# Float64 weights split from the upper word alone, magnitudes made one piece ahead, and layer 1's sets of seven products in another order

## The chip, the cores and the metric

The kernel runs on one core of a Trainium2 chip. The metric is the device time of one execution in microseconds (us), median of three runs. Five engines matter: TensorE (PE, the matmuls, and PEld, its weight loads), VectorE (DVE), ScalarE (ACT), GpSimd (POOL) and the DMA queue of SyncE (SP). Each engine takes its own instructions in the order in which the program was written, and waits on semaphores where it needs another engine's result.

## The reference

```python
attn_out = retention(q, k, v)              # float32, 4 x 8 heads x 576 x 64
x = attn_out as (2304, 512)
h = x @ moe_w_in                           # float64 weights, 512 x 2048
x = (max(h, 0) ** 2) @ moe_w_out           # the first block: float64 weights, 2048 x 512
p = probs / (probs.sum(-1) + 1e-9)         # 2304 x 4
out = sum over e of p[:, e] * (max(x @ w1[e], 0) @ w2[e])   # the second block, float32 weights
```

Matmul operands are float32 numbers held as a high and a low part (names ending in `hi` and `lo`), and every product is three matmuls: high by high, high by low, low by high.

## The kernel before

Three stages follow each other: attention (0 to 79 us), the first block (79 to 520 us) and the second block. The change touches the first block alone.

**Chunks and jobs.** The first block takes the 2048 hidden columns in eight chunks `c` of 256 (`NW1`). The 2304 tokens stand in five groups `g`, four of 512 and one of 256. A list `jobs`, written out by hand, gives the order: a layer 1 job for chunk and group, then the layer 2 jobs of an earlier layer 1 (`behind`). Layer 2 (`layer2_1`) multiplies the hidden values `ghi`/`glo` by `w2hi`/`w2lo` into a bank `o` and VectorE adds that to the sums `y` (L860).

**Sets of seven.** For chunks 2 to 5 (`sevens`) two groups of 512 tokens (a pair) go through layer 1 together as a two-by-two block product with seven instead of eight products (`layer1_seven`). Each chunk has two such calls, eight in all. A product is six matmuls of 512 columns (L658). The seven results stand in four PSUM banks `b1`, `b6`, `b7`, `b5`; `b1`, `b7` and `b5` each take a second product on top of the first one. Before that, the first result must have been read: `b1` by ScalarE's copy to `u[0]` (L677), `b7` and `b5` by VectorE's `add` (L666). At the end of each of the four sums stands `square`: Relu (L589) and Square (L591) on ScalarE, then `split`: ScalarE's copy to the high part (L123) and GpSimd's subtraction for the low part (L124).

**Weights in the background.** The weights of the first block arrive as float64. Each chunk has eight pieces of 128x256 doubles: four for layer 1 (`split_w1`) and four for layer 2 (`split_w2`). `load_piece` fetches them into three rotating buffers `wraw`. `from_f64` turns one piece into `hi` and `lo`: Abs of the upper word on ScalarE (L105), four VectorE operations on the exponent (L107 to L113), a fifth that scales the lower word (L115), GpSimd's sum of the two (L116), then `split`. In chunks 2 to 5 `split_w1` also makes the four sums S1 to S4 of the quarters A11 to A22 that the seven products need.

These are Python generators in a list `work`. After every product and every layer 2 tile, `tick(n)` runs `n` steps of the first generator, a step being the code between two `yield`s. That alone decides where a step's instructions stand in each engine's queue. `combine`, which makes four differences of the tokens (T1 to T4) for each pair and saves them to memory, is a generator in the same list, during chunks 0 and 1. Before a job, `drain` runs whatever is left of the weights that the job needs. `pull` issues the loads that bring the saved differences back (L611).

Of the kernel before, what the change touches and what calls it, by code (L numbers as in the profile page):

```python
# [28 lines left out]
BC = 256  # L29
# [4 lines left out]
def tile_kernel(ctx, tc, qT, kT, kn, vn, v4d, mask, qdec, kdec, wd, w, probs, probs2, out, outT):  # L34
# [33 lines left out]
    def f32(ap):  # L68
        return ap.bitcast(F32)
# [20 lines left out]
            nc.sync.dma_start(out=r, in_=w[(c - NW1) % NW2][:, 2 * BC * i : 2 * BC * (i + 1)])  # L90
        wraw[c, i] = r

    def from_f64(r, hi, lo):

        n = r.shape[1]
        low, high = r[:, :, 0], r[:, :, 1]
        m = cvp.tile([128, n], I32, name="cv_m", bufs=4)  # L100
        p = cvp.tile([128, n], F32, name="cv_d", bufs=2)
        a = m.bitcast(F32)
        v = nc.vector
        yield
        nc.scalar.activation(out=a, in_=high.bitcast(F32), func=ACTF.Abs)  # L105
        yield
        v.tensor_scalar(out=a, in0=a, scalar1=2.0**-15, scalar2=2.0**16 * 1.875, op0=ALU.max, op1=ALU.min)  # L107
        yield
        v.tensor_scalar(out=m, in0=m, scalar1=5, scalar2=2, op0=ALU.logical_shift_left, op1=ALU.logical_shift_right)
        yield  # L110
        v.scalar_tensor_tensor(out=m, in0=high, scalar=-(1 << 30), in1=m, op0=ALU.bitwise_and, op1=ALU.bitwise_or)  # L111
        yield
        v.tensor_scalar(out=p.bitcast(I32), in0=m, scalar1=-(1 << 23), scalar2=None, op0=ALU.bitwise_and)  # L113
        yield
        v.scalar_tensor_tensor(out=p, in0=low.bitcast(U32), scalar=2.0**-52, in1=p, op0=ALU.mult, op1=ALU.mult)  # L115
        nc.gpsimd.tensor_tensor(out=a, in0=a, in1=p, op=ALU.add)  # L116
        yield
        yield
        split(a, hi, lo)
        return a  # L120

    def split(src, hi, lo):
        nc.scalar.copy(out=hi, in_=src)  # L123
        nc.gpsimd.tensor_tensor(out=lo, in0=src, in1=f32(hi), op=ALU.subtract)  # L124
# [7 lines left out]
    def split_w1(c):  # L132

        hi = wp.tile([128, 8 * BC], F32R, name="w1hi")
        lo = wp.tile([128, 8 * BC], F32R, name="w1lo")
        blk = [slice(BC * i, BC * (i + 1)) for i in range(8)]
        if c < NW1:

            w1s[c] = [t.rearrange("p (i k m) -> p i k m", i=8, k=2) for t in (hi, lo)]
            u, v = {}, nc.vector  # L140
            for i, to in ((2, A21), (3, A22), (0, A11), (1, A12)):
                r = wraw.pop((c, i))
                u[to] = yield from from_f64(r, hi[:, blk[to]], lo[:, blk[to]])
                load_piece()
                if c not in sevens:
                    continue
                if to == A11:
                    yield
                    v.tensor_tensor(out=u[A22], in0=u[A21], in1=u[A22], op=ALU.add)
                    yield  # L150
                    v.tensor_tensor(out=u[A21], in0=u[A11], in1=u[A21], op=ALU.subtract)
                    split(u[A22], hi[:, blk[S1]], lo[:, blk[S1]])
                    yield
                    v.tensor_tensor(out=u[A11], in0=u[A22], in1=u[A11], op=ALU.subtract)
                    split(u[A21], hi[:, blk[S3]], lo[:, blk[S3]])
                    yield
                    split(u[A11], hi[:, blk[S2]], lo[:, blk[S2]])
                if to == A12:
                    yield
                    v.tensor_tensor(out=u[A12], in0=u[A12], in1=u[A11], op=ALU.subtract)  # L160
                    yield
                    split(u[A12], hi[:, blk[S4]], lo[:, blk[S4]])
            return
        w1t[c] = hi, lo
        w1s[c] = [t.rearrange("p (i k m) -> p i k m", i=8, k=2) for t in (hi, lo)]
        r0, r1 = wraw.pop((c, 0)), wraw.pop((c, 1))
        a11, a12, a21, a22 = r0[:, :BC], r0[:, BC:], r1[:, :BC], r1[:, BC:]
        v = nc.vector
        s = [cvp.tile([128, BC], F32, name="cv_m", bufs=4) for _ in range(4)]
        todo = [  # L170
            (s[0], a21, a22, ALU.add), (s[1], s[0], a11, ALU.subtract), (s[2], a11, a21, ALU.subtract),
            (s[3], a12, s[1], ALU.subtract),
        ]
        src = {A11: a11, A12: a12, A22: a22, A21: a21, S1: s[0], S2: s[1], S3: s[2], S4: s[3]}
        for i in (A11, S2, S3, A12, S1, A22, S4, A21):
            for _ in range(2 if todo else 0):
                yield
                o, x, y, op = todo.pop(0)
                v.tensor_tensor(out=o, in0=x, in1=y, op=op)
            yield  # L180
            split(src[i], hi[:, blk[i]], lo[:, blk[i]])
            if i in (A12, A21):
                load_piece()
# [12 lines left out]
    def split_w2(c):  # L196

        whole = NW1 <= c < NW1 + NW2 - 1
        new_w2(c, whole)
        blk = lambda y, i: w2b(c, y, i, i + 1)  # L200
        if c < NW1:
            for i in range(4):
                r = wraw.pop((c, 4 + i))
                yield from from_f64(r, blk(0, i), blk(1, i))
                load_piece()
            return
        r = wraw.pop((c, 2)), wraw.pop((c, 3))
        a = [r[i // 2][:, BC * (i % 2) : BC * (i % 2 + 1)] for i in range(4)]
        v = nc.vector
        t = [cvp.tile([128, BC], F32, name="cv_m", bufs=4) for _ in range(4)]  # L210
        todo = [
            (t[0], a[H21], a[H22], ALU.add), (t[1], t[0], a[H11], ALU.subtract), (t[2], a[H21], a[H11], ALU.subtract),
            (t[3], a[H12], t[1], ALU.subtract),
        ]
        for piece in ((H11, H21), (H12, H22)):
            for i in piece:
                yield
                split(a[i], blk(0, i), blk(1, i))
            for _ in range((3 if piece[0] == H11 else 1) if whole else 0):
                yield  # L220
                o, x, y, op = todo.pop(0)
                v.tensor_tensor(out=o, in0=x, in1=y, op=op)
            load_piece()
        for i in range(4 if whole else 0):
            yield
            split(t[i], blk(0, 4 + i), blk(1, 4 + i))
# [298 lines left out]
    with tc.manual_schedule():  # L525
# [62 lines left out]
        def square(h, r, hi, lo, act=True):  # L588
            nc.scalar.activation(out=r, in_=h, func=ACTF.Relu)  # L589
            if act:  # L590
                nc.scalar.activation(out=r, in_=r, func=ACTF.Square)  # L591
            else:
                nc.vector.tensor_tensor(out=r, in0=r, in1=r, op=ALU.mult)
            split(r, hi, lo)

        T1, T2, T3, T4 = range(4)
        parted, bufs, pulls = {}, {}, []
# [1 line left out]
        def pull():  # L599
            if pulls:  # L600
                pulls.pop(0)()
# [15 lines left out]
        def combine(pair):  # L617

            s = 4 * pair
            raw, half = [t.rearrange("p (i n) -> p i n", i=2) for t in bufs["raw"]], bufs["half"]  # L620
            v = nc.vector
            for k in range(2):
                r = {}
                for n, i in enumerate((s, s + 2, s + 3, s + 1)):
                    r[i - s] = raw[n // 2][:, n % 2, :]
                    yield
                    nc.gpsimd.tensor_tensor(
                        out=r[i - s], in0=f32(slot(xh_, i)[:, k, :]), in1=f32(slot(xl_, i)[:, k, :]), op=ALU.add
                    )
                b11, b21, b12, b22 = (r[i] for i in range(4))  # L630
                for i, o, x, y in ((T1, b11, b12, b11), (T3, b12, b22, b12), (T2, b11, b22, b11), (T4, b21, b21, b11)):
                    yield
                    v.tensor_tensor(out=o, in0=x, in1=y, op=ALU.subtract)
                    yield
                    j = bufs["n"] % 2
                    bufs["n"] += 1
                    hi, lo = (t[:, j, :] for t in half)
                    nc.scalar.copy(out=hi, in_=o)
                    v.tensor_tensor(out=lo, in0=o, in1=f32(hi), op=ALU.subtract)
                    yield  # L640
                    for y_, t in enumerate((hi, lo)):
                        nc.sync.dma_start(out=saved(pair, i, y_)[:, k, :], in_=f32(t))

        def layer1_seven(c, ga, gb):
# [9 lines left out]
            def product(o, i, x, first=True):  # L654
                n = 0
                for k in range(2):
                    for a, y in ((w1h, 0), (w1h, 1), (w1l, 0)):
# [2 lines left out]
                            skip_group_check=True,  # L660
                        )
                        n += 1
                tick(3)

            def add(o, x, y):
                v.tensor_tensor(out=o, in0=x, in1=y, op=ALU.add)  # L666
# [11 lines left out]
            b6 = bank()  # L678
            product(b6, S2, bufs[T2])
            add(u[1], b6, u[0])  # L680
            product(b1, A12, own(1), False)
            square(b1, u[0], ha[:, 0, :], la[:, 0, :])
            b7 = bank()
            product(b7, S3, bufs[T3])
            add(u[2], b7, u[1])
            pull()
            b5 = bank()
            product(b5, S1, bufs[T1])
# [622 lines left out]
```

## Time and profile before

| | us |
|---|---|
| median of three runs | 1320.66 (1319.97 to 1322.03) |
| the profiled execution, own time | 1321.92 |
| its span, first to last instruction | 1320.1 |
| PE busy in the span | 1223.6 (93%) |
| DVE, ACT, POOL busy | 921.2, 480.2, 706.7 |
| mean granted TensorE clock | 0.972 |

The profile shows one execution. The span leaves 1.8 us of the execution's own time outside. Busy shares are means over stages that are limited in different ways, so the views of single stretches say more: the wait view tells how long an engine stood idle and which instruction of which engine released it, and the timeline gives start and length of each instruction.

### The profile page before, as it was taken

What the parts mean: (1) busy time and instruction counts of PE and PEld (TensorE: products, weight loads), DVE (VectorE), ACT (ScalarE), POOL (GpSimd) and SP (SyncE); (2) the same over time, 40 slices, a digit from 0 to 9 for tenths busy, and PEclk for the clock granted to TensorE, in tenths of its full rate; (3) what the DMA queues carried; (4) which work ended last, traced back from release to release, by engine and by line L of the source; (5) the groups of instructions that cost most, each with busy time, mean ns of one, the idle gap of its engine ahead of it and who ended that gap; (6) DMA issues with size and microseconds to landing.
All of it is one profiled execution on the core that took longest, in us unless ns stands there. A gap on an engine that the chain in (4) does not pass through costs nothing.

```text
span 1320.1 us, 18475 instructions
## 1 busy us (share of the span) xinstructions
PE 1223.6 (93%) x6422; PEld 1012.0 (77%) x6422; DVE 921.2 (70%) x1558; ACT 480.2 (36%) x1122; POOL 706.7 (54%) x721
## 2 busy tenths in 40 slices
PE   7998786787888899999999999999999999999997
PEld 6877564666766688878888888788787888888876
DVE  4775576676765665866677677866785787777768
ACT  4644544443433323454333343333431222222221
POOL 5645564544443443454444444453524777777775
PEclk9999897998899999999999999999999999999999
DMA  9932346554544310025534552454569556645641
GB/s 338 312 110 72 128 152 230 194 178 169 184 168 159 111 34 16 17 80 207 216 144 150 214 209 86 180 220 169 207 217 350 183 168 215 214 163 181 223 159 65
DMA packets 93537, 224.26 MB, mean 170 GB/s; under 512 B 11266, under 2 KB 19970, under 8 KB 93444
## 3 DMA queue, kind: packets, MB, share of 16 engines
q1 hardware_dynamic: 92932, 222.38, 47.6%
q8 instruction: 51, 0.84, 0.3%
q10 hardware_dynamic: 512, 0.70, 0.2%
q14 instruction: 42, 0.34, 0.1%
HBM read 149.88 MB, written 73.16 MB: 169 GB/s over the span
## 4 chain that ended last, share of the span: by engine, by line
PE 61%; DVE 16%; ACT 8%; issue 6%; POOL 5%; DMA 4%; ACTq 0%; SPq 0%; DVEq 0%; POOLq 0%
PE o L884 14%; PE h L935 10%; PE h L1017 10%; PE h L722 10%; PE h L574 7%; PE o L852 5%; POOL cv_m L116 2%; DVE cv_m L107 2%; DVE cv_m L111 1%; ACT ghi L123 1%; DVE cv_d L115 1%; PE h L658 1%; DVE y L860 1%; DVE cv_d L113 1%; DVE xl L811 1%
## 5 line engine op out<-in xcount | busy, mean ns | idle before, releaser
L124 POOL TENSOR_TENSOR glo<-r,ghi 128x512 fp32r<-128x512 f32 (+1 forms) x72 | 86.9, 1207 | 105.9 <-ACT ghi L123 91.8
L852 PE MATMUL o<-ghi,w2hi 128*128 128x512 f32 (+1 forms) x320 | 123.3, 385 | 9.9 <-ACT w2hi L123 3.8
L892 DVE SCALAR_TENSOR_TENSOR oacc<-o,pr,oacc 128x512 f32<-128x512 f32 x150 | 109.8, 744 | 29.8 <-PE o L884 29.5
L852 PE MATMUL o<-glo,w2hi 128*128 128x512 f32 (+1 forms) x320 | 123.2, 385 | 7.8 <-POOL glo L124 7.8
L1027 DVE TENSOR_TENSOR sums<-sums,h 128x512 f32<-128x512 f32 x202 | 128.4, 677 | 2.7 <-PE h L1017 2.7
L884 PE MATMUL o<-w2hi,ghi 128*128 128x512 f32 x320 | 124.9, 390 | 0.5 <-ACT w2hi L123 0.4
L884 PE MATMUL o<-w2lo,ghi 128*128 128x512 f32 x320 | 124.7, 390 | 0.6 <-POOL w2lo L124 0.6
L884 PE MATMUL o<-w2hi,glo 128*128 128x512 f32 x320 | 124.7, 390 | 0.0
L852 PE MATMUL o<-ghi,w2lo 128*128 128x512 f32 (+1 forms) x320 | 122.4, 382 | 0.5 <-POOL w2lo L124 0.5
L116 POOL TENSOR_TENSOR cv_m<-cv_m,cv_d 128x256 f32<-128x256 f32 x64 | 48.7, 761 | 108.3 <-DVE cv_d L115 108.3
L124 POOL TENSOR_TENSOR w1lo<-cv_m,w1hi 128x256 fp32r<-128x256 f32 x112 | 86.5, 779 | 37.1 <-ACT w1hi L123 37.1
L574 PE MATMUL h<-xh,w1hi 128*128 128x256 f32 (+1 forms) x320 | 104.6, 327 | 1.5 <-DVE xl L464 0.8
L124 POOL TENSOR_TENSOR w2lo<-wraw,w2hi 128x256 fp32r<-128x256 f32 x64 | 52.1, 841 | 98.8 <-ACT w2hi L123 98.8
L574 PE MATMUL h<-xh,w1lo 128*128 128x256 f32 (+1 forms) x320 | 104.2, 325 | 0.0
L574 PE MATMUL h<-xl,w1hi 128*128 128x256 f32 (+1 forms) x320 | 104.2, 325 | 0.0
L107 DVE TENSOR_SCALAR cv_m<-cv_m 128x256 f32<-128x256 f32 x64 | 41.9, 654 | 81.1 <-ACT cv_m L105 80.9
L860 DVE TENSOR_TENSOR y<-o,y 128x512 f32<-128x512 f32 (+1 forms) x140 | 85.8, 628 | 13.0 <-PE o L852 12.9
L935 PE MATMUL h<-xh,w1hi 128*128 128x512 f32 x224 | 88.5, 395 | 3.8 <-ACT r L954 2.6
L722 PE MATMUL h<-xh,w1hi 128*128 128x512 f32 x224 | 88.3, 394 | 2.1 <-ACT r L735 1.1
L722 PE MATMUL h<-xh,w1lo 128*128 128x512 f32 x224 | 88.0, 393 | 2.2 <-POOL w1lo L124 2.2
L935 PE MATMUL h<-xh,w1lo 128*128 128x512 f32 x224 | 87.9, 392 | 0.2 <-DMA w1lo<-kept 0.2
L722 PE MATMUL h<-xl,w1hi 128*128 128x512 f32 x224 | 87.7, 392 | 0.0
(199 smaller groups left out, 3211.8 us busy)
## 6 DMA issues: line engine op xcount, KB each, us to landing
wraw<-wd SPq DMA_DIRECT2D x64, 256.0 KB, 2.8
wraw<-w SPq DMA_DIRECT2D x64, 256.0 KB, 3.0
xh<-parted SPq DMA_DIRECT2D x16, 512.0 KB, 4.6
xl<-parted SPq DMA_DIRECT2D x16, 512.0 KB, 5.5
r2hi<-parted SPq DMA_DIRECT2D x16, 512.0 KB, 5.4
r2lo<-parted SPq DMA_DIRECT2D x16, 512.0 KB, 5.5
kept<-w1hi SPq DMA_DIRECT2D x16, 512.0 KB, 5.2
kept<-w1lo SPq DMA_DIRECT2D x16, 512.0 KB, 5.9
```

Source lines behind the costliest of these rows:

```text
L107: v.tensor_scalar(out=a, in0=a, scalar1=2.0**-15, scalar2=2.0**16 * 1.875, op0=ALU.max, op1=ALU.min)
L116: nc.gpsimd.tensor_tensor(out=a, in0=a, in1=p, op=ALU.add)
L124: nc.gpsimd.tensor_tensor(out=lo, in0=src, in1=f32(hi), op=ALU.subtract)
L574: nc.tensor.matmul(h, wk(a, f, k), group(x, g, k), start=(n == 0), stop=(n == 3 * KT - 1))
L722: nc.tensor.matmul(o, a[:, i, k, :], slot(x, j)[:, k, :], start=(first and n == 0), stop=(n == 5), skip_group_check=True,)
L852: nc.tensor.matmul(o, a[:, f, 128 * m : 128 * m + 128], x[:, f, :], start=(n == 0), stop=(n == 3 * FT - 1))
L860: nc.vector.tensor_tensor(out=y, in0=o, in1=y, op=ALU.add)
L884: nc.tensor.matmul(o, a[:, f, 128 * m : 128 * m + 128], x[:, f, :], start=(n == 0), stop=(n == 3 * FT - 1))
L892: nc.vector.scalar_tensor_tensor(out=acc, in0=o, scalar=pr[:, tt, e : e + 1], in1=acc, op0=ALU.mult, op1=ALU.add)
L935: nc.tensor.matmul(o, a[:, i, k, :], slot(x, j)[:, k, :], start=(first and n == 0), stop=(n == 5), skip_group_check=True,)
L1017: nc.tensor.matmul(b, w2b(c, a, i, i + 1)[:, 128 * d : 128 * d + 128], o[x][:, y, :], start=(first and n == 0), stop=(n == 2), skip_group_ ...
L1027: v.tensor_tensor(out=e, in0=e, in1=b, op=op)
```

## The change

Six things differ.

- `from_f64`: the copy to `hi` is taken from the upper word's value, right after the fourth VectorE operation, before the lower word is added. GpSimd's sum and its subtraction for `lo` then stand next to each other. A piece takes six steps instead of eight.
- The Abs of the next piece is issued behind that copy, if the piece has been loaded (`magnitudes`).
- `split_w1`: S2 and S4 get a buffer `s2` of their own from the pool of `cv_d`, and the steps around them change places.
- `layer1_seven`: `tick(2)` instead of `tick(3)` after a product; the A12 product and its `square` go behind the S3 product; that `square` gets `b1` as source and as place for its result.
- `square`: where its result is written over its source (`r is h`), the low part is subtracted on VectorE instead of GpSimd. Four of the calls in `layer1_seven` pass the same tile twice: the one on `b1`, and those on `u[2]`, `u[0]` and `u[1]`.
- `combine`: one more `yield`, between ScalarE's copy and VectorE's subtraction.

```diff
+    doubles = [x for x in pieces if x[0] < NW1]
+    magnitudes = {}
+
+    def absolute(key, r):
+        m = cvp.tile([128, BC], I32, name="cv_m", bufs=4)
+        nc.scalar.activation(out=m.bitcast(F32), in_=r[:, :, 1].bitcast(F32), func=ACTF.Abs)
+        return m
...
-        m = cvp.tile([128, n], I32, name="cv_m", bufs=4)
+        m = magnitudes.pop(key) if key in magnitudes else absolute(key, r)
         p = cvp.tile([128, n], F32, name="cv_d", bufs=2)
         a = m.bitcast(F32)
         v = nc.vector
-        yield
-        nc.scalar.activation(out=a, in_=high.bitcast(F32), func=ACTF.Abs)
         yield
...
         v.tensor_scalar(out=p.bitcast(I32), in0=m, scalar1=-(1 << 23), scalar2=None, op0=ALU.bitwise_and)
+        nc.scalar.copy(out=hi, in_=a)
+        i = doubles.index(key) + 1
+        if i < len(doubles) and doubles[i] in wraw:
+            magnitudes[doubles[i]] = absolute(doubles[i], wraw[doubles[i]])
         yield
         v.scalar_tensor_tensor(out=p, in0=low.bitcast(U32), scalar=2.0**-52, in1=p, op0=ALU.mult, op1=ALU.mult)
+        yield
         nc.gpsimd.tensor_tensor(out=a, in0=a, in1=p, op=ALU.add)
-        yield
-        yield
-        split(a, hi, lo)
+        nc.gpsimd.tensor_tensor(out=lo, in0=a, in1=f32(hi), op=ALU.subtract)
         return a
...
                 if to == A11:
+                    s2 = cvp.tile([128, BC], F32, name="cv_d", bufs=2)
                     yield
                     v.tensor_tensor(out=u[A22], in0=u[A21], in1=u[A22], op=ALU.add)
                     yield
+                    split(u[A22], hi[:, blk[S1]], lo[:, blk[S1]])
                     v.tensor_tensor(out=u[A21], in0=u[A11], in1=u[A21], op=ALU.subtract)
-                    split(u[A22], hi[:, blk[S1]], lo[:, blk[S1]])
                     yield
-                    v.tensor_tensor(out=u[A11], in0=u[A22], in1=u[A11], op=ALU.subtract)
                     split(u[A21], hi[:, blk[S3]], lo[:, blk[S3]])
+                    v.tensor_tensor(out=s2, in0=u[A22], in1=u[A11], op=ALU.subtract)
                     yield
-                    split(u[A11], hi[:, blk[S2]], lo[:, blk[S2]])
+                    split(s2, hi[:, blk[S2]], lo[:, blk[S2]])
                 if to == A12:
                     yield
-                    v.tensor_tensor(out=u[A12], in0=u[A12], in1=u[A11], op=ALU.subtract)
                     yield
-                    split(u[A12], hi[:, blk[S4]], lo[:, blk[S4]])
+                    v.tensor_tensor(out=s2, in0=u[A12], in1=s2, op=ALU.subtract)
+                    yield
+                    split(s2, hi[:, blk[S4]], lo[:, blk[S4]])
...
-            split(r, hi, lo)
+            if r is h:
+                nc.scalar.copy(out=hi, in_=r)
+                nc.vector.tensor_tensor(out=lo, in0=r, in1=f32(hi), op=ALU.subtract)
+            else:
+                split(r, hi, lo)
...
                     nc.scalar.copy(out=hi, in_=o)
+                    yield
                     v.tensor_tensor(out=lo, in0=o, in1=f32(hi), op=ALU.subtract)
...
-                tick(3)
+                tick(2)
...
             add(u[1], b6, u[0])
-            product(b1, A12, own(1), False)
-            square(b1, u[0], ha[:, 0, :], la[:, 0, :])
             b7 = bank()
             product(b7, S3, bufs[T3])
             add(u[2], b7, u[1])
+            product(b1, A12, own(1), False)
+            square(b1, b1, ha[:, 0, :], la[:, 0, :])
             pull()
```

The order of instructions shows it at one call of `layer1_seven`, that of chunk 3 on the second pair of groups. On VectorE before, from the `add` of `b7` (its result is `cv_tp`) to the last `add` of the call, with rows L107 to L115 being steps of `from_f64`:

```order
L666 TENSOR_TENSOR cv_tp<-h,r 128x512
L107 TENSOR_SCALAR cv_m<-cv_m 128x256
L666 TENSOR_TENSOR cv_tp<-h,cv_tp 128x512
L109 TENSOR_SCALAR cv_m<-cv_m 128x256
L111 SCALAR_TENSOR_TENSOR cv_m<-wraw,cv_m 128x256
L113 TENSOR_SCALAR cv_d<-cv_m 128x256
L666 TENSOR_TENSOR r<-h,r 128x512
L115 SCALAR_TENSOR_TENSOR cv_d<-wraw,cv_d 128x256
L666 TENSOR_TENSOR r<-h,r 128x512
```

On VectorE now, in the same call, from the subtraction for the `b1` result on. L606 is the subtraction in `square`, L681 is `add`, and L114 to L126 are the steps of `from_f64`:

```order
L606 TENSOR_TENSOR glo<-h,ghi 128x512
L120 TENSOR_SCALAR cv_d<-cv_m 128x256
L126 SCALAR_TENSOR_TENSOR cv_d<-wraw,cv_d 128x256
L681 TENSOR_TENSOR cv_tp<-h,cv_tp 128x512
L606 TENSOR_TENSOR glo<-cv_tp,ghi 128x512
L114 TENSOR_SCALAR cv_m<-cv_m 128x256
L681 TENSOR_TENSOR r<-h,r 128x512
L606 TENSOR_TENSOR glo<-r,ghi 128x512
L116 TENSOR_SCALAR cv_m<-cv_m 128x256
L118 SCALAR_TENSOR_TENSOR cv_m<-wraw,cv_m 128x256
L681 TENSOR_TENSOR r<-h,r 128x512
L606 TENSOR_TENSOR glo<-r,ghi 128x512
```

Four subtractions that GpSimd did have come in, and three of them stand directly behind the `add` whose result ScalarE still has to square and copy.

On ScalarE before, around the copy of `b1` to `u[0]` (L677) in that call; L123 is a copy to a high part, L105 an Abs, L589 and L591 are Relu and Square:

```order
L105 ACTIVATE cv_m<-wraw 128x256
L123 CAST w1hi<-cv_m 128x256
L677 COPY r<-h 128x512
L123 CAST w1hi<-cv_m 128x256
L105 ACTIVATE cv_m<-wraw 128x256
L589 ACTIVATE r<-h 128x512
L591 ACTIVATE r<-r 128x512
L123 CAST ghi<-r 128x512
```

On ScalarE now, around the same copy (L692); L121 is the copy to a weight's high part, L98 the Abs of the next piece:

```order
L121 CAST w2hi<-cv_m 128x256
L98 ACTIVATE cv_m<-wraw 128x256
L692 COPY r<-h 128x512
L121 CAST w2hi<-cv_m 128x256
L98 ACTIVATE cv_m<-wraw 128x256
L599 ACTIVATE h<-h 128x512
L601 ACTIVATE h<-h 128x512
L605 CAST ghi<-h 128x512
```

The weights are further along at this call (layer 2's pieces instead of layer 1's), each copy to a high part is followed at once by the next piece's Abs, and the copy waits for VectorE where it waited for GpSimd.

## Rows read from the trace of the kernel before

**Rows 1.** The page: busy us and share of the span by engine.

```profile
PE 1223.6 (93%) x6422; PEld 1012.0 (77%) x6422; DVE 921.2 (70%) x1558; ACT 480.2 (36%) x1122; POOL 706.7 (54%) x721
```

**Rows 2.** Busy time by stage: stretch, its length, busy us by engine, granted clock, DMA.

```profile
122.00:206.00 84.00, 59.74 (x238) 47.20 (x236) 53.37 (x83) 36.38 (x74) 45.81 (x41) 0.85 0.42 153
206.00:440.00 234.00, 191.84 (x854) 154.98 (x855) 151.12 (x303) 98.29 (x210) 108.52 (x126) 0.92 0.49 177
440.00:560.00 120.00, 119.27 (x568) 99.39 (x566) 83.52 (x148) 45.10 (x91) 51.16 (x51) 0.99 0.11 36
```

**Rows 3.** Waits of PE from 75 to 440 us: total us, times, longest.

```profile
PE h L658 <- ACT r L677: 23.6, 7, 5.9
PE h L658 <- DVE cv_tp L666: 15.8, 9, 3.4
PE h L658 <- ACT w1hi L123: 9.1, 1, 9.1
PE o L852 <- POOL glo L124: 6.8, 6, 3.4
PE o L852 <- ACT w2hi L123: 3.8, 1, 3.8
```

**Rows 4.** Waits of DVE from 206 to 440 us.

```profile
DVE cv_m L107 <- ACT cv_m L105: 53.0, 33, 4.7
DVE y L860 <- PE o L852: 10.6, 10, 3.6
DVE cv_m L160 <- POOL w1lo L124: 10.4, 4, 4.8
```

**Rows 5.** Waits of ACT from 206 to 440 us.

```profile
ACT w2hi L123 <- POOL cv_m L116: 51.3, 15, 8.8
ACT w1hi L123 <- POOL cv_m L116: 43.9, 17, 4.2
```

**Rows 6.** Groups of DVE instructions, 206 to 440 us: busy us, mean ns, idle before.

```profile
L107 DVE TENSOR_SCALAR cv_m<-cv_m 128x256 f32<-128x256 f32 x36 | 24.2, 672 | 53.1 <-ACT cv_m L105 53.0
...
L666 DVE TENSOR_TENSOR r<-h,r 128x512 f32<-128x512 f32 x22 | 15.0, 683 | 0.1
```

**Rows 7.** Timeline: the longest wait for ACT's copy (start, us, instruction, idle before).

```profile
309.37 0.72 POOL L116 TENSOR_TENSOR cv_m<-cv_m,cv_d 128x256 f32<-128x256 f32 x1 [2.01 <-DVE cv_d L115]
...
310.13 0.40 ACT L123 CAST w1hi<-cv_m 128x256 fp32r<-128x256 f32 x1 [3.27 <-POOL cv_m L116]
310.44 0.58 ACT L677 COPY r<-h 128x512 f32<-128x512 f32 x1
...
311.07 0.80 PE L658 MATMUL h<-xh,w1hi 128*128 128x512 f32 x1 [5.92 <-ACT r L677]
```

**Rows 8.** Timeline: from one add over ACT's square to GpSimd's subtraction.

```profile
319.32 0.68 DVE L666 TENSOR_TENSOR cv_tp<-h,cv_tp 128x512 f32<-128x512 f32 x1
...
320.03 0.63 ACT L589 ACTIVATE cv_tp<-cv_tp 128x512 f32<-128x512 f32 x1 [1.25 <-DVE cv_tp L666]
...
321.36 0.62 ACT L123 CAST ghi<-cv_tp 128x512 fp32r<-128x512 f32 x1
...
322.05 1.30 POOL L124 TENSOR_TENSOR glo<-cv_tp,ghi 128x512 fp32r<-128x512 f32 x1 [2.81 <-ACT ghi L123]
```

**Rows 9.** Timeline: like DVE instructions with and without a GpSimd one beside them.

```profile
182.66 3.41 POOL L627 TENSOR_TENSOR raw_r2lo<-xh,xl 128x512 f32<-128x512 f32 x2
...
184.87 1.75 DVE L633 TENSOR_TENSOR raw_r2hi<-raw_r2lo,raw_r2hi 128x512 f32<-128x512 f32 x1
...
190.23 0.68 DVE L633 TENSOR_TENSOR raw_r2lo<-raw_r2lo,raw_r2hi 128x512 f32<-128x512 f32 x1
...
192.86 0.28 DVE L107 TENSOR_SCALAR cv_m<-cv_m 128x256 f32<-128x256 f32 x1
```

**Rows 10.** Timeline of SP's queue: the last load before chunk 2's first call.

```profile
205.69 0.42 SPq L611 DMA_DIRECT2D xl<-parted  x1
```

**Rows 11.** The page's DMA issues: KB each, median us to landing.

```profile
xl<-parted SPq DMA_DIRECT2D x16, 512.0 KB, 5.5
```

More of the change, by code (lines that the diff above doesn't have):

```diff
@@ L91, in load_piece, with from_f64 @@
         wraw[c, i] = r
-    def from_f64(r, hi, lo):
+    doubles = [x for x in pieces if x[0] < NW1]
[4 more added lines that the diff above has]
+        return m
+    def from_f64(key, hi, lo):
+        r = wraw.pop(key)
         n = r.shape[1]
         low, high = r[:, :, 0], r[:, :, 1]
-        m = cvp.tile([128, n], I32, name="cv_m", bufs=4)
+        m = magnitudes.pop(key) if key in magnitudes else absolute(key, r)
         p = cvp.tile([128, n], F32, name="cv_d", bufs=2)
@@ L141, in split_w1 @@
             for i, to in ((2, A21), (3, A22), (0, A11), (1, A12)):
-                r = wraw.pop((c, i))
-                u[to] = yield from from_f64(r, hi[:, blk[to]], lo[:, blk[to]])
+                u[to] = yield from from_f64((c, i), hi[:, blk[to]], lo[:, blk[to]])
                 load_piece()
@@ L202, in split_w2 @@
             for i in range(4):
-                r = wraw.pop((c, 4 + i))
-                yield from from_f64(r, blk(0, i), blk(1, i))
+                yield from from_f64((c, 4 + i), blk(0, i), blk(1, i))
                 load_piece()
```

## The prediction

> **What bounds the kernel now.** I read the page's shares first. PE is busy for 1223.6 of 1320.1 us [rows 1], so 96.5 us is all that shorter waits could give back, apart from the clock. Next I asked where these 96.5 us are, with busy time by stage. From 206 to 440 us, where chunks 2 to 5 go through the sets of seven, PE is busy for 191.8 of 234 us at a mean granted clock of 0.92; from 122 to 206 us it is 59.7 of 84 us at 0.85; from 440 us on it is hardly ever idle [rows 2]. So the change works in the two stretches in which 66 us are idle, and the reader can forget the rest.
>
> Then the wait view says for whom. Up to 440 us PE stood 23.6 us in seven waits for ScalarE's copy of `b1`, 15.8 us in nine waits for VectorE's `add`, 9.1 us once for a high part of chunk 2's weights, and 3.8 us once for a high part of layer 2's weights [rows 3]. One timeline shows how such a wait comes about. The longest, 5.92 us before the A12 product, ended with a copy of 0.58 us; what was late was not the copy but what stood ahead of it on ScalarE, a weight's copy to the high part that had been held for 3.27 us by GpSimd's sum L116, which itself had waited for VectorE [rows 7]. This pattern is general: in the stage of the sevens ScalarE stood 51.3 + 43.9 us in such copies, for that sum [rows 5], and VectorE stood 53.0 us waiting for an Abs that ScalarE reached late [rows 4]. VectorE itself is busy for 151.1 of the 234 us [rows 2]. So the stage is bound by a ring of short waits between three engines that take instructions in order, not by the work of one.
>
> **The change, part by part.** *High part from the upper word.* ScalarE's copy no longer waits for GpSimd. It stays as long as it was. The 95 us of held ScalarE time are not on PE's path as a whole; what of them is, is in PE's 23.6 us.
>
> *Magnitudes a piece ahead.* The Abs stands two VectorE steps ahead of its user, so I let VectorE's 53.0 us go. A wait for a piece's load could come in its place on ScalarE, with the copy of `b1` behind it. The loads go out three pieces ahead, and VectorE's waits [rows 4] name no load, so I price it at nothing; the cover is at least one whole piece.
>
> *Six steps a piece, two a product.* Fewer steps run under the seven products, but less is to be done. With the steps counted off the code, a chunk needs 55 instead of 70. Those of chunk 2's layer 1 weights are then through before the job ahead of chunk 2's first call, where now the last of them run only when PE already stands there. The single wait of 9.1 us [rows 3] should fall to about 2 us (bounds 0 and 9.1). The layer 2 weights of chunk 1 move forward in the same way, so the 3.8 us go. Together 7.1 + 3.8 = 10.9 us. `combine`'s extra `yield` costs steps, no instruction.
>
> *A12 behind S3.* One more product (six matmuls) now lies between ScalarE's copy and A12, and between the `add` of `b7` and A22. Nothing more lies between the `add` of `b5` and S4.
>
> *One result kept in its bank.* Here the code does more than that. The test `r is h` holds for all four squares of a call, so 8 x 4 = 32 subtractions go from GpSimd to VectorE. The eight on `b1` find their square mostly done, since other steps stand ahead of them. The other 24 stand directly behind the `add` that ScalarE's chain starts from. In the trace that `add` ends at 319.32 + 0.68 = 320.00 and the subtraction starts at 322.05 [rows 8]; 2.05 us, with VectorE free for other steps in between. Now it is held: behind it stand the next `add`, the weights' steps and the sums of `y`.
>
> So VectorE becomes the engine to add up. For the stage from 206 to 440 us, to the same point in the program (the last call's S4 product):
>
> - busy now 151.1 us [rows 2];
> - 32 subtractions of 0.683 us, the duration of an `add` of that size [rows 6]: +21.9;
> - 24 holds of 2.05 us: +49.2;
> - less crowding with GpSimd: L107 takes 672 ns on the mean [rows 6] and 0.28 us when nothing is in its way [rows 9], so 36 x 0.39 = 14.1 us is the most that can go. I take half, -7, because GpSimd keeps its short instructions and loses the long ones (1.30 us, [rows 8]);
> - what comes behind S4 in the last call (three holds and five instructions, 6.15 + 3.4): -9.6;
> - waits for PE and for GpSimd, 10.6 + 10.4 now [rows 4], of which I keep 8 (bounds 0 and 21).
>
> That is 213.6 us, against 234. The gain is 20.4 us, and VectorE bounds the stage. It is far less than the 48 us of idle PE in the first three of PE's waits [rows 3] suggest, because 71 us come onto VectorE where 53 + 13 go.
>
> One rule speaks against the moved subtractions. The row first: the same VectorE subtraction with both inputs in SBUF took 0.68 us alone and 1.75 us while GpSimd worked beside it [rows 9]. The Trainium skill, "SBUF — State Buffer", section "SBUF: two separate sides", says that VectorE and GpSimd share a port pair that one of them holds for a whole instruction, and that a VectorE instruction with two SBUF inputs needs it. The trace agrees. What this would make of the time is a rival, below.
>
> **Sum.** 10.9 + 20.4 = 31.3 us. The profiled execution took 1321.92 us, 1.3 above the median; 1321.9 - 31.3 = 1290.6, and against the median 1289.3. I say 1289. I leave the clock out of the sum: if it had been 1.0 in both stretches, PE would have had 0.15 x 59.7 + 0.08 x 191.8 = 24 us less to do at most, but where VectorE bounds the stage that buys nothing.
>
> **The rivals.** *A: as summed*, 1278 to 1301: the crowding term between 0 and -14, the kept waits between 0 and 15, the wait ahead of chunk 2 between 0 and 5 us. Chance 0.53.
>
> *B: the shared port.* The 24 subtractions with both inputs in SBUF each meet a GpSimd instruction of 0.72 us [rows 7]: +17 us, 1306. For it: 1.75 against 0.68 us [rows 9]. Against: GpSimd is busy for 108.5 of 234 us now and loses the longer instructions, so most meet nothing. Chance 0.15. The rule of the Trainium skill cited above ("SBUF — State Buffer", "SBUF: two separate sides") has the loser wait for the whole instruction. The trace agrees in 1.75 against 0.68 us.
>
> *C: PE becomes the bound.* The holds fall into time in which VectorE had nothing else to do, the 23.6 us and half of the 15.8 us go, and half of the 24 us of clock comes back: 31.5 + 10.9 + 12 = 54 us, 1266. For it: in layer 2 VectorE can lag by some banks without harm. Against: the sum above. Chance 0.13.
>
> *D: slower.* In `square`, ScalarE's Relu stands behind whatever was put into its queue before. If a hold on VectorE contains another chain (three ScalarE instructions of 0.63, 0.63 and 0.62 us [rows 8]) it takes 4 instead of 2.05 us, and 24 of them add 47 us: 1336. The time passes the old one when a hold takes 2.05 + 31.3 / 24 = 3.4 us. Against: VectorE does not reach the next `add` before the chain ahead is done. Chance 0.09.
>
> *E: the change does not do what it says.* Chunk 2's first call waits for something else than weights. The last load of the saved differences goes out at 205.69 us [rows 10] and lands 5.5 us later [rows 11], at about 211 us, when the stage of the sevens has been running since 206 [rows 2]; if it doesn't move, the 9.1 us stay, and with a busier VectorE half the 20.4 us too: 1289 + 7 + 10 = 1306. If the rest of the 20.4 goes as well, it's 1317, no change. Chance 0.10.
>
> **How the numbers follow.** About 2.6 us (0.2%) is what can be told from no change. A gives faster, C faster, B nearly always; E splits 0.07 faster, 0.03 same; D 0.08 slower, 0.01 same; 0.02 of B is same. Faster 0.53 + 0.13 + 0.13 + 0.07 = 0.86, same 0.06, slower 0.08. The range leaves out D and the better half of C and has to take in B and E: 1268 to 1312. A's own range is 1278 to 1301.
>
> **What would show it.** The waits of PE for the copy of `b1` should fall from 23.6 us to under 6, and the wait before chunk 2 to about 2 us. PE's waits for the `add` in cv_tp should stay near 15 us or grow. On VectorE the Abs should vanish as releaser, and ScalarE's copy `ghi` should come up as the new one with about 49 us in 24 waits. ScalarE's waits for GpSimd's sum should be gone. The prediction is wrong if these holds are much shorter or longer than 2 us, if VectorE's busy time in the stage is not some 165 us, or if PE waits for loads.

## The result and the profile after

The changed kernel takes 1297.51 us (median of four runs, 1295.70 to 1297.58), the kernel before 1321.18 us in the runs beside them. The ratio is 0.982, with a 95% interval of 0.980 to 0.984. That is 23.7 us faster, where 31.3 us had been forecast.

The profiled execution took 1295.70 us, 26.2 us less than the profiled one of before, and some 1.8 us less than the other three runs. To compare stages I cut both traces at the same two places of the program: the first matmul of chunk 2 (the A11 product of its first call), and the first matmul of the last call's S4 product. Before:

```profile
206.16 0.79 PE L658 MATMUL h<-xh,w1hi 128*128 128x512 f32 x1 [9.10 <-ACT w1hi L123]
...
441.50 0.70 PE L658 MATMUL h<-xh,w1hi 128*128 128x512 f32 x1
```

The second place is at 441.5 us and not at 440, where [rows 2] end: the six matmuls from 439.61 us on still belong to A22. Now:

```profile
195.67 0.40 PE L673 MATMUL h<-xh,w1hi 128*128 128x512 f32 x1
...
418.39 0.50 PE L673 MATMUL h<-xh,w1hi 128*128 128x512 f32 x1 [1.17 <-DVE cv_tp L681]
```

Busy time by stage, columns as in [rows 2]; first the stage of the sevens before, then three stretches of the changed kernel, the first of them from 122 us, as there:

```profile
206.20:441.50 235.30, 193.31 (x859) 155.87 (x859) 152.23 (x305) 98.21 (x210) 108.99 (x127) 0.92 0.49 176
...
122.00:195.70 73.70, 63.55 (x277) 50.58 (x278) 53.21 (x79) 34.96 (x71) 39.01 (x35) 0.91 0.39 142
195.70:418.40 222.70, 190.66 (x861) 154.22 (x859) 162.41 (x337) 102.48 (x218) 75.68 (x99) 0.92 0.56 197
418.40:540.00 121.60, 120.14 (x576) 100.39 (x577) 90.68 (x153) 46.04 (x93) 49.53 (x50) 1.00 0.11 35
```

Chunk 2 starts at 195.7 instead of 206.2 us: 10.5 us gained, although the first block itself starts 1.7 us later (81.1 instead of 79.4 us). The stage of the sevens takes 222.7 instead of 235.3 us: 12.6 us gained. (An expectation below counts it as 220.7 us, from the call's second product at 197.71 us on.) From there to the end it is 1293.9 - 418.4 = 875.5 instead of 1320.1 - 441.5 = 878.6 us, another 3.1 us. Of these, 1.1 us lie in the S4 product itself. Before, its matmuls stood behind a wait of 3.37 us ahead of A22 and ran at a granted clock of 0.51, the lower of TensorE's two levels (1.2 of 2.4 GHz); now, behind a wait of 1.17 us, they run at 1.00:

```profile
441.50:444.10 2.60, 2.60 (x7) 2.05 (x7) 0.79 (x2) 2.54 (x6) 0.76 (x2) 0.51 0.67 222
...
418.40:419.90 1.50, 1.50 (x6) 1.23 (x7) 0.00 (x0) 1.38 (x3) 0.94 (x2) 1.00 0.49 108
```

PE's waits up to 440 us, against [rows 3]:

```profile
PE h L673 <- DVE cv_tp L681: 11.2, 10, 2.7
PE h L673 <- ACT r L692: 10.0, 4, 4.0
PE o L867 <- ACT y L873: 7.5, 6, 3.7
PE o L867 <- ACT ghi L133: 6.4, 4, 2.7
PE o L867 <- POOL glo L134: 5.0, 6, 1.5
PE h L584 <- ACT y L873: 2.5, 2, 2.2
```

The single waits of 9.1 us and 3.8 us for weights are gone, the waits for the copy of `b1` (now L692) fell from 23.6 to 10.0 us, those for the `add` (now L681) from 15.8 to 11.2 us. New are 10.0 us for chunk 0's layer 2 results `y`, where one wait of 3.6 us stood before.

VectorE's waits in the stage of the sevens, against [rows 4]:

```profile
DVE glo L606 <- ACT ghi L605: 48.7, 27, 2.1
DVE y L875 <- PE o L867: 3.3, 6, 0.7
DVE cv_d L171 <- POOL cv_m L128: 3.1, 3, 1.9
```

The 53.0 us for the Abs have left the list, and 48.7 us for the copy `ghi` have come in. PE is hardly waited for any more (3.3 against 10.6 us): VectorE is the engine that is late. ScalarE's waits in the same stage, against [rows 5]:

```profile
ACT w1hi L121 <- DVE cv_m L118: 33.2, 13, 3.7
ACT w2hi L121 <- DVE cv_m L118: 27.4, 12, 6.8
```

GpSimd's sum is not among them; the copies to the high part now wait for VectorE. The timeline of one call (chunk 3, first pair) shows two of the holds:

```profile
276.81 0.68 DVE L681 TENSOR_TENSOR cv_tp<-h,cv_tp 128x512 f32<-128x512 f32 x1
...
277.53 0.63 ACT L599 ACTIVATE cv_tp<-cv_tp 128x512 f32<-128x512 f32 x1 [0.26 <-DVE cv_tp L681]
...
278.85 0.62 ACT L605 CAST ghi<-cv_tp 128x512 fp32r<-128x512 f32 x1
279.51 0.69 DVE L606 TENSOR_TENSOR glo<-cv_tp,ghi 128x512 fp32r<-128x512 f32 x1 [2.02 <-ACT ghi L605]
...
280.45 0.68 DVE L681 TENSOR_TENSOR r<-h,r 128x512 f32<-128x512 f32 x1
...
281.50 0.74 POOL L129 TENSOR_TENSOR w1lo<-cv_m,w1hi 128x256 fp32r<-128x256 f32 x1
...
283.15 0.69 DVE L606 TENSOR_TENSOR glo<-r,ghi 128x512 fp32r<-128x512 f32 x1 [2.02 <-ACT ghi L605]
```

VectorE ends an `add`, stands for 2.02 us while ScalarE runs Relu, Square and copy, subtracts for 0.69 us, and does the same again after the next `add`.

### The profile page after: what moved, and what is told of

Read it like the earlier page. It is cut to its first block, busy times and chain, and to the rows that moved or that the text cites. A ratio compares the mean times of both kernels' runs of the same rounds, so it can differ in the third digit from the quotient of the medians.

```text
span 1293.9 us, 18553 instructions
## 1 busy us (share of the span) xinstructions
PE 1218.5 (94%) x6422; PEld 1008.4 (78%) x6422; DVE 943.7 (73%) x1590; ACT 480.4 (37%) x1122; POOL 669.1 (52%) x689
## 5 line engine op out<-in xcount | busy, mean ns | idle before, releaser
L134 POOL TENSOR_TENSOR glo<-r,ghi 128x512 fp32r<-128x512 f32 (+1 forms) x48 | 56.4, 1178 | 90.2 <-ACT ghi L133 80.6
L737 PE MATMUL h<-xl,w1hi 128*128 128x512 f32 x224 | 87.6, 391 | 0.0
L950 PE MATMUL h<-xl,w1hi 128*128 128x512 f32 x224 | 87.5, 391 | 0.0
L867 PEld LDWEIGHTS o<-ghi,w2hi 128*128 128x128 f32 x320 | 63.0, 197 | 28.0 <-ACT y L873 9.9
```

Source lines behind the costliest of these rows:

```text
L737: nc.tensor.matmul(o, a[:, i, k, :], slot(x, j)[:, k, :], start=(first and n == 0), stop=(n == 5), skip_group_check=True,)
L867: nc.tensor.matmul(o, a[:, f, 128 * m : 128 * m + 128], x[:, f, :], start=(n == 0), stop=(n == 3 * FT - 1))
L950: nc.tensor.matmul(o, a[:, i, k, :], slot(x, j)[:, k, :], start=(first and n == 0), stop=(n == 5), skip_group_check=True,)
```

## The experiments

Theory H, after the result: VectorE bounds the sets of seven, and it does so by standing still behind its own `add`, not by its work. Rival S: the holds lie in time that VectorE had to spare, and it's the short waits of PE that count. Rival W: the work that came over from GpSimd counts.

**pool24.** The 24 subtractions on `u[2]`, `u[0]` and `u[1]` go back to GpSimd.

```diff
-        def square(h, r, hi, lo, act=True):
+        def square(h, r, hi, lo, act=True, bank=False):
...
-            if r is h:
+            if bank:
...
-            square(b1, b1, ha[:, 0, :], la[:, 0, :])
+            square(b1, b1, ha[:, 0, :], la[:, 0, :], bank=True)
```

> The changed kernel, with the 24 subtractions of the in-place squares on u[2], u[0] and u[1] back on GpSimd; only the one on b1 stays on VectorE. Theory H (holds of VectorE bound the sets of seven: 48.7 us of waits for the copy ghi in a stage of 220.7 us): the stage falls to about 200 us, the time to 1275 to 1283 us. Rival S (the holds lie in time that VectorE had to spare, and latencies between engines bound the stage): 1294 to 1300 us, no change. Half a gain (1287 to 1292) would mean that another bound stands close behind.

Measured: 1275.32 us, ratio to the kernel before 0.967 (0.965 to 0.969). The stage of the sevens takes 201.8 instead of 222.7 us. H holds, S falls.

**late24.** The same 24 subtractions stay on VectorE, each issued one product later.

```diff
+        late = []
+
-        def square(h, r, hi, lo, act=True):
+        def square(h, r, hi, lo, act=True, keep=False):
...
-                nc.vector.tensor_tensor(out=lo, in0=r, in1=f32(hi), op=ALU.subtract)
+                late.append(lambda: nc.vector.tensor_tensor(out=lo, in0=r, in1=f32(hi), op=ALU.subtract))
+                if not keep:
+                    late.pop()()
...
-            square(u[2], u[2], hb[:, 1, :], lb[:, 1, :])
+            square(u[2], u[2], hb[:, 1, :], lb[:, 1, :], keep=True)
...
+            late.pop()()
-            square(u[0], u[0], ha[:, 1, :], la[:, 1, :])
+            square(u[0], u[0], ha[:, 1, :], la[:, 1, :], keep=True)
...
+            late.pop()()
-            square(u[1], u[1], hb[:, 0, :], lb[:, 0, :])
+            square(u[1], u[1], hb[:, 0, :], lb[:, 0, :], keep=True)
...
+                if m == 1 and late:
+                    late.pop()()
                 tick(pace[0])
```

> The changed kernel, with the same 24 subtractions on VectorE, but each issued one product later (behind the next add; the last one of a call behind the second sum of the next layer 2 job). VectorE's work is the same, the holds go. Theory H: VectorE's waits for ghi fall from 48.7 to about 6 us and the time to 1278 to 1288 us, a few us above the run that moves them to GpSimd. Rival W (the 22 us of work that came onto VectorE is what costs, not the holding): 1294 to 1300 us.

Measured: 1274.60 us, ratio 0.966 (0.965 to 0.967). The stage of the sevens in this run, then its waits on VectorE:

```profile
195.10:396.90 201.80, 182.05 (x861) 148.76 (x859) 164.94 (x338) 101.92 (x218) 78.26 (x99) 0.96 0.61 218
```

```profile
DVE glo L608 <- ACT ghi L607: 14.4, 14, 1.4
DVE y L881 <- PE o L873: 14.1, 14, 3.6
```

VectorE is busy for 164.9 us, no less than in the changed kernel (162.4), yet the stage takes 201.8 instead of 222.7 us. With the holds down from 48.7 to 14.4 us, VectorE waits for PE again. This settles H against W: the same work costs nothing when something else stands between the `add` and the subtraction. The time is 3 us below H's range. Of the 20.9 us that the stage gives back, 8.6 are PE's own busy time: the same matmuls take 182.1 instead of 190.7 us, at a granted clock of 0.96 instead of 0.92, while PE stands less.

**a12_first.** The product A12 and its square go ahead of S3 again.

```diff
+            product(b1, A12, own(1), False)
+            square(b1, b1, ha[:, 0, :], la[:, 0, :])
             b7 = bank()
             product(b7, S3, bufs[T3])
             add(u[2], b7, u[1])
-            product(b1, A12, own(1), False)
-            square(b1, b1, ha[:, 0, :], la[:, 0, :])
```

> The changed kernel with the A12 product ahead of the S3 product again; all else stays. Theory H (VectorE bounds the stage): PE's waits for the copy of b1 grow, but they replace waits for the add, 1296 to 1303 us. Rival O (the order of the products gave most of the gain): eight more waits of about a product each, 8 x 1.4 us, 1306 to 1312 us.

Measured: 1299.04 us, ratio 0.984 (0.983 to 0.986), not told apart from the changed kernel's 0.982. PE's waits mostly change their names: 20.5 us for the copy of `b1` and 6.1 us for the `add`, against 10.0 and 11.2.

**before_held.** The kernel before, with in-place squares on VectorE.

```diff
-            split(r, hi, lo)
+            if r is h:
+                nc.scalar.copy(out=hi, in_=r)
+                nc.vector.tensor_tensor(out=lo, in0=r, in1=f32(hi), op=ALU.subtract)
+            else:
+                split(r, hi, lo)
```

> The kernel before, with one edit: squares written over their source subtract the low part on VectorE (24 in the sets of seven). Theory H: 24 holds of 2 us and 16 us of work are added to a VectorE that is busy for 151 of 234 us and idle mostly because it waits for Abs; the sum, 216 us, is near the stage's length, so part of it shows: 1325 to 1345 us. Rival S (holds in spare time): 1318 to 1324 us. If holds and Abs waits simply add up: up to 1380 us.

Measured: 1335.89 us, ratio 1.012 (1.010 to 1.014), 16 us slower. VectorE's waits in the sevens' stage of this run:

```profile
DVE glo L596 <- ACT ghi L595: 42.8, 21, 2.5
DVE cv_m L107 <- ACT cv_m L105: 31.2, 27, 3.4
```

42.8 us of holds came in, and 21.8 of the 53.0 us of waits for the Abs [rows 4] went. So part of the holds fell into time in which VectorE would have stood anyway. This edit alone is a loss; in the change it was carried by the others.

The next four undo one part of the changed kernel each.

**abs_own_step.** The Abs stands at its own piece's first step again.

```diff
-        m = magnitudes.pop(key) if key in magnitudes else absolute(key, r)
+        yield
+        m = absolute(key, r)
...
-        i = doubles.index(key) + 1
-        if i < len(doubles) and doubles[i] in wraw:
-            magnitudes[doubles[i]] = absolute(doubles[i], wraw[doubles[i]])
```

> The changed kernel with the Abs of a piece at the piece's own first step again (seven steps a piece), all else as changed. Prediction's reading (the Abs ahead frees VectorE of its 53 us of waits, and VectorE bounds the sets of seven): some 35 waits of 0.5 to 1 us come back on VectorE, 1308 to 1325 us. Rival (ScalarE is no longer held by GpSimd, so the Abs is quick wherever it stands): 1294 to 1302 us.

Measured: 1302.08 us, ratio 0.987 (0.984 to 0.989), some 4.6 us behind the changed kernel. What came back is not what I had priced. VectorE waits for an Abs for 7.9 us in the stage, in 8 waits, not some 35. Instead a wait ahead of chunk 2's first call is there again, now that a piece takes seven steps:

```profile
PE h L671 <- ACT w1hi L122: 7.6, 1, 7.6
```

The trace is that of the slowest of the four executions (1306.91 us, the others 1298.80 to 1303.52), and its first block starts at 84.7 us instead of 81.1, so how much of the 4.6 us this wait makes is not shown.

**hi_of_sum.** The copy to the high part stands behind GpSimd's sum again.

```diff
-        nc.scalar.copy(out=hi, in_=a)
         i = doubles.index(key) + 1
...
-        nc.gpsimd.tensor_tensor(out=lo, in0=a, in1=f32(hi), op=ALU.subtract)
+        split(a, hi, lo)
```

> The changed kernel with the copy to the high part taken behind GpSimd's sum again (steps, Abs and order as changed). Prediction's reading: ScalarE is held for GpSimd again, with Relu and Square behind it, so the holds of VectorE get longer: 1303 to 1318 us. Rival (with six steps a piece there is room enough): 1294 to 1301 us.

Measured: 1310.54 us, ratio 0.993 (0.991 to 0.994), 13 us behind. ScalarE's waits in the stage of this run:

```profile
ACT w2hi L132 <- POOL cv_m L127: 44.8, 15, 8.2
ACT w1hi L132 <- POOL cv_m L127: 37.9, 15, 3.8
```

ScalarE is held for GpSimd as in [rows 5], and VectorE's holds grew from 48.7 to 57.4 us. Of the parts undone alone, this is the dearest.

**tick3.** Three steps behind each product of seven.

```diff
-                tick(2)
+                tick(3)
```

> The changed kernel with three steps behind each product of seven again. If VectorE bounds the stage, it makes no difference where its steps stand: 1293 to 1302 us. If the steps between the products delay the adds that PE waits for, PE's waits in the calls grow by up to 7 steps of 0.4 us in each of 8 calls: 1303 to 1320 us.

Measured: 1304.72 us, ratio 0.988 (0.987 to 0.990), 7 us behind. PE's waits for the `add` are 15.5 instead of 11.2 us, and one wait of 3.0 us for a load has come in. So it does matter where the steps stand, though VectorE bounds the stage; which of the two waits counts for how much is not shown.

**no_yield.** `combine` without its extra `yield`.

```diff
                     nc.scalar.copy(out=hi, in_=o)
-                    yield
                     v.tensor_tensor(out=lo, in0=o, in1=f32(hi), op=ALU.subtract)
```

> The changed kernel without the extra yield in combine. It saves 16 steps ahead of chunk 2 and holds VectorE for a copy of 0.62 us 16 times. By the sum (the yield costs steps, no time): 1294 to 1300 us. If the yield is what spared VectorE: 1301 to 1308 us. If it pushes the layer 2 copies of chunk 0 back on ScalarE (10 us of PE's waits for y): 1286 to 1293 us.

Measured: 1302.11 us, ratio 0.986 (0.984 to 0.988), some 4.6 us behind. PE's waits for `y` are 14.6 instead of 10.0 us. Chunk 2 starts at 205.1 instead of 195.7 us, though PE waits for no weight there; the stage of the sevens is then 5.0 us shorter (422.8 - 205.1 = 217.7 us). The step that I had priced at nothing is worth a few us in all, and 9.4 us ahead of chunk 2.

The last four build on pool24.

**pool24_a12_first.** A12 ahead of S3, as in a12_first.

```diff
+            product(b1, A12, own(1), False)
+            square(b1, b1, ha[:, 0, :], la[:, 0, :], bank=True)
             b7 = bank()
...
-            product(b1, A12, own(1), False)
-            square(b1, b1, ha[:, 0, :], la[:, 0, :], bank=True)
```

> The run pool24 with the A12 product ahead of S3 again. Under the holds this order made no difference that could be told (1299 against 1297.5 us). If VectorE's bound hid it, it shows now: PE waits about a product more for the copy of b1 in each call, 8 x 1.0 to 1.4 us, 1283 to 1288 us. If the order is worth nothing in itself: 1273 to 1278 us.

Measured: 1276.65 us, ratio 0.967 (0.965 to 0.969), pool24's own. The new order of the products is worth nothing that can be told, with the holds or without them.

**pool32.** The square of `b1` goes to `u[0]`, its low part to GpSimd.

```diff
-            square(b1, b1, ha[:, 0, :], la[:, 0, :], bank=True)
+            square(b1, u[0], ha[:, 0, :], la[:, 0, :])
```

> The run pool24 with the square of b1 written to u[0] instead of its bank, its low part on GpSimd too. VectorE loses 8 x 0.69 us of work and about 6 us of holds, GpSimd gets 8 x 1.3 us, and the add into u[0] has to wait for GpSimd. If VectorE still sets the pace of the calls: 1266 to 1272 us. If the result kept in its bank is what gives the add free way: 1279 to 1288 us. In between, neither shows.

Measured: 1270.63 us, ratio 0.962 (0.961 to 0.964), below pool24's 0.967 (0.965 to 0.969). The result that is kept in its bank costs some 5 us too. In pool24 VectorE still stood 5.9 us for its `ghi`, and none in pool32; but the edit moves eight subtractions as well, so hold and work are not told apart here.

**pool24_y_dve.** Chunk 0's layer 2 results leave the bank by VectorE.

```diff
-                    nc.scalar.copy(out=y, in_=o)
+                    nc.vector.tensor_copy(out=y, in_=o)
```

> The run pool24 with chunk 0's layer 2 results copied out by VectorE instead of ScalarE. PE waits 10 us for these copies on ScalarE, where they stand behind a copy for combine that waits for VectorE and GpSimd. If ScalarE's queue is the cause: 1264 to 1270 us. If VectorE is held at the same place, by the difference ahead of that copy: 1274 to 1284 us.

Measured: 1276.91 us, ratio 0.967 (0.965 to 0.969), no change. PE waits 9.1 us for the same results, now on VectorE. Whichever engine copies them seems to stand behind `combine`'s differences: VectorE waits 7.8 us for GpSimd's sums ahead of them (100 to 165 us).

**pool32_loads.** In pool32, PE waits for loads in chunk 2's first call. SyncE's queue in pool32 just ahead of it:

```profile
185.80 8.16 SPq L87 DMA_DIRECT2D wraw<-wd  x3
194.06 0.37 SPq L625 DMA_DIRECT2D xh<-parted  x1
194.49 0.42 SPq L625 DMA_DIRECT2D xl<-parted  x1
200.38 0.33 SPq L87 DMA_DIRECT2D wraw<-wd  x1
200.76 0.42 SPq L625 DMA_DIRECT2D r2hi<-parted  x1
```

The load of T3's high part goes out at 200.76 us, behind a weight piece that waited for its buffer.

```diff
                 load_parts(0, [(t, bufs[t]) for t in (T2, T3, T1, T4)])
+                for _ in range(4):
+                    pull()
```

> The run pool32 with the first four loads of saved differences (T2 and T3) issued together ahead of chunk 1's last full job, instead of one by one behind its tiles. In pool32 they stand in SyncE's queue behind loads of weight pieces that wait for a buffer, and PE waits 5.8 us for them in chunk 2's first call. If that queue is the cause: PE's waits for loads go, 1264 to 1268 us. If the loads are late because of what they read or of the memory traffic: 1269 to 1272 us.

Measured: 1269.47 us (five runs, 1266.76 to 1271.55), ratio 0.961 (0.960 to 0.962). It can't be told from pool32. The waits for loads fell from 5.8 to 1.1 us, but one wait of 6.1 us for the copy of `b1` came in their place:

```profile
PE h L673 <- ACT r L692: 7.2, 2, 6.1
```

Ahead of that copy on ScalarE stand three copies of weights to their high parts, which were held for 2.65, 1.60 and 1.31 us by VectorE. Why VectorE is late there is not settled.

## Why the prediction was right

The time lies in the range, and rival A's mechanism is the one that was found; its size was too large: 23.7 us came of the forecast 31.3. Point by point:

**VectorE becomes the bound of the sevens, and gives back about half of what the rest of the change brings.** Shown by pool24 and late24: without the holds the time falls by a further 22 us. The account for the stage against the trace:

| us, VectorE, to the last call's S4 | forecast | measured |
|---|---|---|
| busy | 151.1 + 21.9 - 7 - 3.4 = 162.6 | 162.4 |
| holds | 49.2 - 6.15 = 43.1 | 48.7 |
| waits for PE and GpSimd | 8 | 7.0 |
| without a releaser in the list | 0 | 4.6 |
| sum, the stage's length | 213.6 | 222.7 |

Two terms were mis-sized. The holds on `b1` I put at nothing, and six of them took 6.3 us: they are held for up to 1.4 us, because Relu on the bank begins only when A12 has ended. The 21 holds behind an `add` were as forecast (42.5 us, 2.02 us each). And the 4.6 us in which no releaser is listed stood in the trace of before too: there the stage of 235.3 us holds 152.2 us of work and 78.4 us of listed waits, which leaves 4.7 us. The sum had no term for it. The gain of this stage is 12.6 instead of 20.4 us.

**Ahead of chunk 2.** Forecast 10.9, measured 10.5 us; that they agree so closely is in part luck. Both waits went, and wholly (9.1 + 3.8 us, where I had let 2 us stay), while the first block started 1.7 us later and PE's waits for `y` grew. abs_own_step brings the first wait back with one step more per piece, which speaks for the shorter count of steps; but without `combine`'s `yield`, which I had put at nothing, the weights are in time too and 9.4 us of the gain are gone (no_yield). The first call then starts with smaller waits, and the trace shows two for loads among them:

```profile
197.71 0.50 PE L673 MATMUL h<-xh,w1hi 128*128 128x512 f32 x1 [0.49 <-ACT r L599]
199.28 0.65 PE L673 MATMUL h<-xl,w1hi 128*128 128x512 f32 x1 [1.07 <-DMA xl<-parted]
203.60 0.77 PE L673 MATMUL h<-r2hi,w1hi 128*128 128x512 f32 x1 [1.61 <-DVE y L875]
205.42 0.79 PE L673 MATMUL h<-r2lo,w1hi 128*128 128x512 f32 x1 [1.05 <-DMA r2lo<-parted]
```

So rival E was there in small (2.1 us), and PE's waiting for loads was one of my signs of being wrong. Not forecast at all: PE's waits for chunk 0's layer 2 results `y` grew from 3.6 to 10.0 us. I take it that `combine`, further ahead because pieces take fewer steps, now meets that layer 2; no run tests it.

**A wrong reason.** I let the 53 us of waits for the Abs go because the Abs stands a piece ahead. They also go almost wholly without that (abs_own_step, 7.9 us), as long as ScalarE is not held by GpSimd; and with it they go although ScalarE is held (hi_of_sum). Either edit does it. What the upper word alone brings beyond is ScalarE's free queue, 13 us by hi_of_sum. Also wrong were the nothing for `combine`'s `yield` (some 4.6 us by no_yield) and, in an expectation, that a bound VectorE would not mind one step more behind each product (7 us by tick3). PE's waits for the copy of `b1` were to fall under 6 us and are 10.0; those for the `add` were to stay near 15 us or grow and fell to 11.2. That `ghi` comes to 48.7 us, as said (49), is in part chance, since up to S4 these are 21 long holds and six short ones on `b1`, not 24 long ones. The bounds of rival A's three terms, added up, would give 1272 to 1306 us and not 1278 to 1301.

**The rivals.** B, the shared port: the trace decides against it here. VectorE's 32 subtractions, by source line (shortest, median, longest in ns):

```profile
L606 DVE TENSOR_TENSOR glo<-r,ghi x16: 691/692/693, 222.2 to 427.9; 128x512 fp32r<-128x512 f32 x16
L606 DVE TENSOR_TENSOR glo<-h,ghi x8: 678/692/692, 214.7 to 416.4; 128x512 fp32r<-128x512 f32 x8
L606 DVE TENSOR_TENSOR glo<-cv_tp,ghi x8: 691/692/693, 218.7 to 420.4; 128x512 fp32r<-128x512 f32 x8
```

Not one took longer than alone, though [rows 9] show that such an instruction can. They hardly met: in all 24 cases with both inputs in SBUF GpSimd's last instruction had ended at least 0.9 us before the subtraction began, and only once did another begin within it:

```profile
287.32 0.69 DVE L606 TENSOR_TENSOR glo<-r,ghi 128x512 fp32r<-128x512 f32 x1 [2.01 <-ACT ghi L605]
...
287.67 0.94 POOL L134 TENSOR_TENSOR w1lo<-cv_m,w1hi 128x256 fp32r<-128x256 f32 x1 [2.23 <-ACT w1hi L133]
```

There GpSimd's took longer (0.94 us, against 0.74 us for the like one at 284.70 us). So the trace says nothing against what [rows 9] show, only that B's meetings did not come about. It is not the hold that prevents them. In late24 14 of the 24 are not held at all, and none takes longer than 0.69 us either. GpSimd begins within seven of the 24 (or 0.01 us ahead), and each time it is GpSimd's instruction that ends late, some 1.28 us after the subtraction's start:

```profile
353.65 1.29 POOL L128 TENSOR_TENSOR cv_m<-cv_m,cv_d 128x256 f32<-128x256 f32 x1 [5.30 <-ACT w2hi L121]
353.66 0.68 DVE L608 TENSOR_TENSOR glo<-r,ghi 128x512 fp32r<-128x512 f32 x1
...
355.01 0.74 POOL L129 TENSOR_TENSOR w2lo<-cv_m,w2hi 128x256 fp32r<-128x256 f32 x1
```

So in these places a meeting lengthens GpSimd's work, not VectorE's. That GpSimd begins so seldom ahead of a subtraction may be because it gets its work from VectorE's steps; no run tests that. C, PE as the bound, is what the kernel comes nearer to without the holds (in pool24 VectorE waits 18.9 us for PE in the stage, against 3.3 us), not what the change made of it. D, slower, asked for holds of 3.4 us; none was longer than 2.1 us.

**Left open** are 2.0 of the 3.1 us behind the sevens. Some 0.4 us lie between S4 and 996.0 us (now 971.5 us); the first block, which reaches to 582 us before and not to 520, ends in that stretch, and its last weights are still converted there. The other 1.6 us lie behind it, where the two programs do not differ. The profiled execution is 1.8 us faster than its fellows, so a single trace shows too much.

## What to carry to other kernels

Before you move an instruction to another engine, look at what its queue does while the operands are made: the same 24 subtractions cost 22 us more directly behind the `add` that feeds their chain than one product later or on GpSimd, and those two places can't be told apart (1274.6 and 1275.3 us). A step that holds no instruction of its own, such as `combine`'s `yield`, still moves what stands behind it and should not be priced at nothing. A test such as `r is h` must be read at every call, and an edit that loses alone (1.2% slower on the kernel before) can hide in a change that gains. The best version here keeps the new conversion of the weights and takes back the edit to `square`: 1270.6 us, 3.8% below the kernel before.

## What was not expected of the hardware

Subtractions of the kind that [rows 9] show at 1.75 us beside GpSimd ran at 0.69 us in all 24 cases that had both inputs in SBUF, while GpSimd was busy for a third of the stage (75.7 of 222.7 us). By this share some eight of the 24 (an estimate: a third of them) would have begun beside a GpSimd instruction; none did. Here the busy shares did not tell how often the two engines meet, nor which of them a meeting slows: in late24 it was GpSimd's instruction that took up to 1.29 instead of 0.74 us.
